# Pooled attention and a tanh-shrink MLP on one core: where the loads are queued, and who turns batch 1's keys and queries

## The chip, the core and the metric

The kernel runs on one core of one Trainium2 chip. A core has four compute engines, TensorE (matrix products, PE in the profile), VectorE (DVE), ScalarE (ACT) and GpSimd (POOL), and SyncE (SP), which here only issues DMAs. Each engine works through its own list of instructions in order and waits on semaphores for the others. SP, ACT and POOL can each issue DMAs; all of them are moved by the same 16 DMA engines. Data are worked on in SBUF (128 partitions), matrix products land in PSUM, which has 8 banks of 128 x 512 float32.

The metric is the time on the device in microseconds (us) of one execution. Before the change the median of three runs is 329.83 us (329.11 to 329.89).

## The reference

There are 8 batches, 8 heads, 576 positions and a head dimension of 64. Keys and values are averaged over groups of 8 positions, so there are 72 of them per head. The result of the attention, as 4608 rows of 512, goes through two weight matrices with `h - tanh(h)` between them.

```python
k_p = k.reshape(B, H, Sp, pool, D).mean(axis=3)
v_p = v.reshape(B, H, Sp, pool, D).mean(axis=3)
scores = scale * np.matmul(q, k_p.transpose(0, 1, 3, 2))
scores = scores - np.max(scores, axis=-1, keepdims=True)
attn = np.exp(scores)
attn = attn / (np.sum(attn, axis=-1, keepdims=True) + 1e-09)
attn_out = np.matmul(attn, v_p)
x = attn_out.transpose(0, 2, 1, 3).reshape(B * S, H * D)
h = x @ w_in            # 512 -> 2048
g = h - np.tanh(h)
out = g @ w_out         # 2048 -> 512
```

## The kernel before

**Tiling.** Of the 576 positions of a batch, 512 make four blocks of 128 queries (`s_block`, `av_block`), and the last 64 make a "tail"; the tails of two batches share one block of 128 (`s_tail`, `av_tail`). The MLP runs over nine groups of 512 rows: groups 0 to 7 are the blocks of batches 0 to 7, group 8 is the four blocks of tails. In each group the first product (`h_mms`, line 344, in group 0 `h_mm_pair`, line 363) makes 16 tiles h of 128 x 512; ScalarE takes tanh of each (line 355 or 375), VectorE subtracts (line 356 or 376) and writes gT. The second product (`o_mms`, line 384) makes four row blocks, each of 16 matmuls, in 16 units of four matmuls; a finished block is copied out of PSUM (`o_store`, line 403) and stored by SP.

**Attention of the next batch inside a group.** While group g is multiplied, the attention of batch g+1 is woven in by hand: the list `plan` says after which h tile (numbers below zero, -16 to -1) or o unit (0 to 15) each step stands. "s" is the scores of a block (`s_mms`, line 235, then the maximum and the subtraction on VectorE, lines 249 and 252); "e" is the exponential on ScalarE (line 260) and the turn of E into ET by a DMA on SP's queue (`e_turn_dma`, line 273); "a" is attention times values (`av_mms`, line 299), the division on VectorE (lines 317 and 318), and the turn of the block into xT by a DMA on SP's queue (line 327). Group 0 has its own weave, the loop `for u in range(16)`, with the scores of batch 1 behind units 3, 5 and 7 and the attention from unit 10 on.

**What a batch needs beforehand.** Its k, q and v are loaded as float32 (`load_list`). GpSimd adds the eight positions of a group of keys together (`pool_k`, lines 157, 160, 163, into kd), SP's queue turns kd into kT by DMA (line 200), GpSimd places kT into KB (`k_place_kT`, line 194); ScalarE casts q to bfloat16 (`q_cast`, line 208), and SP's queue turns it into qT by DMA (line 214). GpSimd pools v (`pool_v`, lines 172 to 184, into VB). The tail queries are loaded as float32 (`load_tail`, line 129), cast by GpSimd (line 571, for the first pair line 596) and turned by DMA (lines 590 and 598). From group 1 on, these loads stand on SP's queue, one behind each h tile (the list `todo`); those of k and q of batch 2 are on GpSimd's queue (lines 603 to 605), v and the tail of batch 2 on SP's (line 654).

**The start.** Batch 0's k comes in three pieces on SP's queue (rows 0 to 2, the last 64 rows, rows 2 to 4, in units of 128) and q in two halves on ACT's queue. `k_turn_pe`, `q_turn_pe`, `e_turn_pe` and `x_turn_pe` turn batch 0's tiles by TensorE, with a product by a unit matrix into PSUM and a copy out (lines 220, 485, 282, 336). `fill` (line 419) multiplies zeros, to no effect on the result. GpSimd casts the second half of q of batch 0. GpSimd's queue then carries the loads that cast to bfloat16 on the way: v of batch 0 (held until the 64-row piece of k has landed), the first weights w1 in four pieces (the first held until rows 2 to 4 of k have landed), the second weights w2 in four, and between them v of batch 1. SP's queue loads k, q and the tail of batch 1, held until the second piece of w1 has landed (line 470).

```python
after(load_rows(k_rows, k_raw[1], 1), w1_dmas[1])
load_q(1, q_raw[1])
load_tail(0)
```

**Order.** The order of each engine's instructions, and of each queue's DMAs, is the order in which the program writes them. An engine that waits holds up everything behind it.

Of the kernel before, what the change touches and what calls it, by code (L numbers as in the profile page):

```python
# [27 lines left out]
NT = 5  # L28
# [7 lines left out]
def kernel(  # L36
# [50 lines left out]
    tl_raw = [const.tile([128, H, D], FP32, name=f"tl_raw{i}") for i in range(2)]  # L87
# [39 lines left out]
    def load_tail(i, eng=None):  # L127
        for s in range(2):
            (eng or nc.sync).dma_start(
                out=tl_raw[i % 2][64 * s : 64 * s + 64, :, :],  # L130
                in_=q[2 * i + s, :, QA:S, :].rearrange("h p d -> p h d"),
            )

# [19 lines left out]
    def pool_k(b, eng, t0=0, t1=NT):  # L153
        r = k_raw[b % 2].rearrange("p t (j d) -> p t j d", d=D)[:, t0:t1, :, :]
        kd = kds[b % 2][:, t0:t1, :, :]
        n = t1 - t0
        eng.tensor_tensor(  # L157
            out=r[:, :, 0:4, :], in0=r[:, :, 0:4, :], in1=r[:, :, 4:8, :], op=ALU.add
        )
        eng.tensor_tensor(  # L160
            out=r[:, :, 0:2, :], in0=r[:, :, 0:2, :], in1=r[:, :, 2:4, :], op=ALU.add
        )
        eng.tensor_tensor(
            out=kd,
            in0=r[:, :, 0:1, :].to_broadcast([128, n, 2, D]),
            in1=r[:, :, 1:2, :].to_broadcast([128, n, 2, D]),
            op=ALU.add,
        )
# [258 lines left out]
    load_rows(k_rows, k_raw[0], 0, 0, 2)  # L427
# [42 lines left out]
    after(load_rows(k_rows, k_raw[1], 1), w1_dmas[1])  # L470
    load_q(1, q_raw[1])
    load_tail(0)


# [4 lines left out]
    def q_turn_pe(b, j, bank, eng):  # L479
        for m in range(NHP):  # L480
            turn(
                PS[:, bank, m * 128 : (m + 1) * 128],
                q_bf[b % 2][:, j, 2 * m : 2 * m + 2, :].rearrange("p h d -> p (h d)"),
            )
        eng(out=qTs[b % 2][:, j, :, :].rearrange("p m c -> p (m c)"), in_=PS[:, bank, :])
# [82 lines left out]
    def prepare(b):  # L568
        pool_k(b, nc.gpsimd)
        if b % 2:  # L570
            ge(out=tl_bf[(b // 2) % 2][:, :, :], in_=tl_raw[(b // 2) % 2][:, :, :])

    def load_list(b, eng):
        i = b % 2
        r = [
            lambda: load_rows(k_rows, k_raw[i], b, 0, 4, eng),
            lambda: load_rows(k_rows, k_raw[i], b, 4, NT, eng),
            lambda: load_q(b, q_raw[i], eng=eng),
            lambda: load_rows(v_rows, v_raw[i], b, 0, 4, eng),
            lambda: load_rows(v_rows, v_raw[i], b, 4, NT, eng),  # L580
        ]
        if b % 2 == 0:
            r.append(lambda: load_tail(b // 2, eng))
        return r

    def turns(b):
        k_turn_dma(b)
        q_turn_dma(b)
        if b % 2:
            nc.sync.dma_start_transpose(  # L590
                out=tl_T[(b // 2) % 2][:, :, :],
                in_=tl_bf[(b // 2) % 2].rearrange("p h d -> p (h d)"),
            )

    k_place_kT(1, ge)
    ge(out=tl_bf[0][:, :, :], in_=tl_raw[0][:, :, :])
    nc.gpsimd.memset(v_raw[0][64:128, 4, :], 0.0)
    nc.sync.dma_start_transpose(
        out=tl_T[0][:, :, :], in_=tl_bf[0].rearrange("p h d -> p (h d)")
    )  # L600


    for ld in load_list(2, nc.gpsimd)[:3]:
        ld()
# [20 lines left out]
    for u in range(16):  # L625
# [14 lines left out]
        if 10 <= u <= 12:  # L640
            a_unit(u - 10, av_block(1), (PB, PA, PB)[u - 10], (1, u - 10))
        if u == 12:
            k_turn_dma(2)
        if u == 13:
            av_mms(ets[3], av_block(1), PA)
            x3 = normalise(PA)
            s_unit(4, s_tail(0), PB)
        if u == 14:
            x_turn_pe(x3, 1, 3, 0, se)
            e_unit(4)  # L650
            tail0 = ets[4]
        if u >= 12:
            o_store(0, u % 4, OB[u % 4], (se, ve)[u % 2])
    for ld in load_list(2, nc.sync)[3:]:
        ld()
    nc.gpsimd.memset(v_raw[1][64:128, 4, :], 0.0)
    k_place_kT(2, ge)
# [6 lines left out]
    for g in range(1, NG):  # L664
# [4 lines left out]
        if nb is not None:  # L669
# [36 lines left out]
            if g > 1:  # L706
                pool_v(nb, nc.gpsimd)
# [15 lines left out]
        todo = load_list(nb + 1, nc.sync) if more else []  # L723
        for i in range(NHID):
            h_mms(g, i, i % 6)
            h_act(i, i % 6)
            if todo and (g > 1 or i > 4):
                todo.pop(0)()
            if g == 1 and i == 5:
# [3 lines left out]
            if g == 1 and i < 4:  # L733
                q_cast(2, se, i, i + 1)
            if g == 1 and i == 3:
# [48 lines left out]
```

## Time and profile before

| what | us |
|---|---|
| median of three runs | 329.83 |
| the profiled execution | 331.36 |
| its span, first to last instruction | 329.6 |
| TensorE busy | 298.8 (91% of the span) |
| VectorE busy | 191.6 (58%) |
| ScalarE busy | 149.8 (45%) |
| GpSimd busy | 108.2 (33%) |
| mean granted TensorE clock | 0.984 |

The profile is of one execution. In its chain of work that ended last, 55% of the span is TensorE and 36% is DMA, of which 12% is ET, 8% the loads of q, 6% qT and 4% xT. In the answers quoted below, a group or a row of the timeline has its start, its length, the engine, the line, and the tiles written and read (written<-read); "idle before" names what ended the wait. A row of the stages has the window, then the busy time of PE, PEld (weight loads of TensorE), DVE, ACT and POOL with the number of instructions, then the granted clock of TensorE (1.00 is full), the busy share of the DMA engines, and GB/s.

### The profile page before, as it was taken

To read this page: it belongs to the slowest core of one execution; us is meant where nothing else is said; L and a number is where in the kernel's file an instruction comes from. 1 tells how busy PE (TensorE), PEld (TensorE's weight loads), DVE (VectorE), ACT (ScalarE), POOL (GpSimd) and SP (SyncE) were. 2 spreads that over 40 slices of the span, in tenths; PEclk is the share of its full clock that TensorE was granted. 3 is DMA by queue.
4 is the path that set the end of the run, shared out by engine and by line. 5 is a ranking of instruction groups with operands and counts; after the bars stand their busy time and mean duration, and the time that the engine had idled before them with its cause. 6 is when DMAs were issued, how large, how long until landed. Compare 5 with 4: busy or idle time off the path is not lost.

```text
span 329.6 us, 4754 instructions
## 1 busy us (share of the span) xinstructions
PE 298.8 (91%) x1737; PEld 149.9 (45%) x1737; DVE 191.6 (58%) x315; ACT 149.8 (45%) x249; POOL 108.2 (33%) x94
## 2 busy tenths in 40 slices
PE   5879959899949799899999999999899989999995
PEld 1347824444415345444454444445444534444443
DVE  5576456578813398349735973696189627505700
ACT  3157452176331474447436733674265316425611
POOL 2831613711770565036707720574090000000000
PEclk9999997999978999999999999999999999999999
DMA  8999997889994899789968995998642360021023
GB/s 232 184 218 270 230 182 225 159 197 238 261 297 97 162 284 212 130 171 266 247 150 209 331 162 139 166 328 184 152 111 38 93 173 7 0 77 52 0 47 81
DMA packets 91735, 55.72 MB, mean 169 GB/s; under 512 B 65504, under 2 KB 79200, under 8 KB 91712
## 3 DMA queue, kind: packets, MB, share of 16 engines
q1 hardware_dynamic: 83440, 46.64, 59.8%
q0 software_dynamic: 6032, 7.60, 12.1%
q10 hardware_dynamic: 2240, 1.18, 1.4%
q8 instruction: 13, 0.21, 0.3%
q14 instruction: 10, 0.08, 0.1%
HBM read 36.70 MB, written 9.44 MB: 140 GB/s over the span
## 4 chain that ended last, share of the span: by engine, by line
PE 55%; DMA 36%; ACT 2%; SPq 2%; issue 1%; DVE 1%; POOL 0%; ACTq 0%
PE PS L344 26%; PE PS L384 24%; DMA ET<-E 12%; DMA q_raw<-in_q_dram 8%; DMA qT<-q_bf 6%; DMA xT<-x_sb 4%; PE PS L299 3%; DMA w1b<-in_moe_w_in_dram 3%; DMA k_raw<-in_k_dram 3%; PE PS L235 2%; ACT q_bf L208 1%; DMA out_dram<-o_sb 1%; SPq L118 1%; DVE mx L249 0%; SPq L405 0%
## 5 line engine op out<-in xcount | busy, mean ns | idle before, releaser
L384 PE MATMUL PS<-w2b,gT 128*128 128x512 bf16 (+2 forms) x592 | 138.1, 381 | 0.0
L356 DVE TENSOR_TENSOR gT<-PS,t_sb 128x512 bf16<-128x512 f32 x128 | 85.7, 689 | 53.0 <-ACT t_sb L355 52.3
L344 PE MATMUL PS<-xT,w1b 128*128 128x512 bf16 x448 | 99.8, 380 | 4.7 <-DMA xT<-x_sb 4.7
L355 ACT ACTIVATE t_sb<-PS 128x512 f32<-128x512 f32 x128 | 76.3, 597 | 39.7 <-PE PS L344 37.2
L384 PEld LDWEIGHTS <-gT 128*128 128x128 bf16 x592 | 55.1, 99 | 58.1 <-issue 3.8
L344 PEld LDWEIGHTS <-w1b 128*128 128x128 bf16 x512 | 49.3, 98 | 63.6 <-issue 6.7
L403 ACT COPY o_sb<-PS 128x512 f32<-128x512 f32 x33 | 19.3, 585 | 84.0 <-PE PS L384 84.0
L260 ACT ACTIVATE E<-sh 128x576 bf16<-128x576 f32 x36 | 24.2, 681 | 27.2 <-DVE sh L252 27.2
L194 POOL COPY KB<-kT 64x288 bf16<-64x288 bf16 x14 | 5.9, 422 | 90.4 <-DMA kT<-kd 73.1
L249 DVE TENSOR_REDUCE mx<-PS 128x8 f32<-128x576 f32 x36 | 27.1, 752 | 10.6 <-PE PS L235 10.5
L317 DVE RECIPROCAL rden<-PS 128x8 f32<-128x8 f32 x36 | 7.4, 206 | 41.4 <-PE PS L299 41.2
L157 POOL TENSOR_TENSOR k_raw<-k_raw 128x1280 f32<-128x1280 f32 x7 | 20.3, 2898 | 27.2 <-DMA k_raw<-in_k_dram 27.2
L299 PE MATMUL PS<-VB,ET 128*128 128x130 bf16 (+4 forms) x240 | 20.3, 227 | 9.5 <-DMA ET<-E 9.5
L252 DVE TENSOR_TENSOR sh<-PS,mx 128x576 f32<-128x576 f32 x36 | 27.3, 758 | 1.3
L318 DVE TENSOR_TENSOR x_sb<-PS,rden 128x512 bf16<-128x512 f32 x36 | 24.9, 692 | 1.4 <-DVE rden L317 0.2
L299 PEld LDWEIGHTS <-ET 128*128 128x128 bf16 (+1 forms) x240 | 15.7, 103 | 20.3 <-DMA ET<-E 14.4
L172 POOL TENSOR_TENSOR v_raw<-v_raw 128x1280 f32<-128x1280 f32 x6 | 17.4, 2902 | 9.9 <-DMA v_raw<-in_v_dram 9.5
L208 ACT CAST q_bf<-q_raw 128x1024 bf16<-128x1024 f32 (+1 forms) x19 | 16.5, 866 | 6.9 <-DMA q_raw<-in_q_dram 6.9
L235 PE MATMUL PS<-KB,qT 128*128 128x144 bf16 x128 | 13.3, 227 | 5.3 <-DMA qT<-q_bf 4.0
L363 PE MATMUL PS<-xT,w1b 128*128 128x256 bf16 x128 | 14.9, 273 | 1.5 <-DVE gT L376 0.8
L235 PEld LDWEIGHTS <-qT 128*128 128x128 bf16 x128 | 9.7, 98 | 13.6 <-DMA qT<-q_bf 5.5
L376 DVE TENSOR_TENSOR gT<-PS,t_sb 128x512 bf16<-128x512 f32 x16 | 10.6, 688 | 7.9 <-ACT t_sb L375 6.3
(66 smaller groups left out, 154.5 us busy)
## 6 DMA issues: line engine op xcount, KB each, us to landing
out_dram<-o_sb SPq DMA_DIRECT2D x32, 256.0 KB, 2.6
k_raw<-in_k_dram SPq DMA_DIRECT2D x6, 1024.0 KB, 6.9
q_raw<-in_q_dram SPq DMA_DIRECT2D x6, 1024.0 KB, 9.3
v_raw<-in_v_dram SPq DMA_DIRECT2D x6, 1024.0 KB, 11.6
w1b<-in_moe_w_in_dram POOLq DMA_DIRECT2D x4, 512.0 KB, 8.9
w2b<-in_moe_w_out_dram POOLq DMA_DIRECT2D x4, 512.0 KB, 23.1
k_raw<-in_k_dram SPq DMA_DIRECT2D x2, 512.0 KB, 6.2
q_raw<-in_q_dram ACTq DMA_DIRECT2D x2, 512.0 KB, 7.4
```

The source lines that it names most:

```text
L157: eng.tensor_tensor(out=r[:, :, 0:4, :], in0=r[:, :, 0:4, :], in1=r[:, :, 4:8, :], op=ALU.add)
L208: eng(out=q_bf[b % 2][:, j0:j1, :, :].rearrange("p j h d -> p h j d"), in_=q_raw[b % 2][:, :, j0:j1, :],)
L235: nc.tensor.matmul(PS[ps, banks[m // 2], KP * (m % 2) : KP * (m % 2) + KP], lhsT=qT[:, m, :], rhs=KB[kb][:, m, :], start=True, stop=True,)
L249: nc.vector.reduce_max(out=mx.rearrange("p k h o -> p k (h o)"), in_=sc, axis=AX.X)
L252: nc.vector.tensor_tensor(out=sh[:, :, :, :], in0=sc, in1=mx.to_broadcast([128, 2, 4, G]), op=ALU.subtract)
L260: nc.scalar.activation(out=E.rearrange("p t c -> p (t c)")[:, 0:NK], in_=sh.rearrange("p k h c -> p (k h c)"), func=ACT.Exp, scale=SCALE,)
L299: nc.tensor.matmul(PS[ps, banks[half], D1 * h : D1 * (h + s1 - s0)], lhsT=ET[:, t, c0 : c0 + (ps.stop - ps.start)], rhs=VB[kb][:, t, s0:s1 ...
L318: nc.vector.tensor_tensor(out=x_sb[:, :, :, :], in0=ps[:, :, :, 0:D], in1=rden.to_broadcast([128, 2, 4, D]), op=ALU.mult,)
L344: nc.tensor.matmul(PS[:, bank, c0:c1], lhsT=w1b[:, fb, i * 128 : (i + 1) * 128], rhs=xT_of(g)[:, fb, c0:c1], start=(fb == 0), stop=(fb == ...
L355: nc.scalar.activation(out=t_sb[:, :], in_=PS[:, bank, :], func=ACT.Tanh)
L356: nc.vector.tensor_sub(out=gT[:, i, :], in0=PS[:, bank, :], in1=t_sb[:, :])
L384: nc.tensor.matmul(PS[:, bank, 0 : c1 - c0], lhsT=gT[:, i, tb * 128 : (tb + 1) * 128], rhs=w2b[:, i, c0:c1], start=(i == 0), stop=(i == NH ...
```

## The change

1. *Start.* Batch 0's k rows 2 to 4 go second on SP's queue, the 64-row piece moves to ACT's queue behind the first half of q, and the second half of q moves from ACT's to SP's queue. v of batch 0 is held until rows 0 to 2 of k have landed, the first piece of w1 is held by nothing, the other three until VectorE has pooled batch 0's keys. ScalarE instead of GpSimd casts the second half of q, ahead of the key placement. The ten fill matmuls ahead of the last key turns become three.
2. *Batch 1.* Its k and q are loaded on GpSimd's queue, behind w1 and ahead of w2; v of batch 1, the last two pieces of w2 and the first tail follow behind the pooling of its keys. In group 0's first product ScalarE casts q behind pairs 6 to 9 (it was 4 to 7), TensorE turns q behind pairs 8 to 11 and k behind the last, ScalarE copies the turned q out, and VectorE and ScalarE place k. The DMAs that turned k and q of batch 1 and GpSimd's placement go.
3. *Tails.* `load_tail` casts on the way, on GpSimd's queue, straight into tl_bf; tl_raw and GpSimd's casts go.
4. *Group 0 and 1.* Block 2 of batch 1 is turned into xT by TensorE and ScalarE instead of by DMA. The tail scores move from unit 13 of group 0 to tile 2 of group 1, their exponential to tile 4, their attention from tile 5 to tile 10; the placement of batch 2's keys follows the tail scores; the casts of batch 2's q move from tiles 0 to 3 to tiles 4 to 7, and their turn from tile 3 to 7.
5. *Later batches.* All loads of a batch are issued on GpSimd's queue: those of batch 2 ahead of the pooling of its keys in group 0, those of batch 3 behind the pooling of v of batch 2, and from group 2 on ahead of the pooling of v at the start of the group.

```diff
-    k0 = load_rows(k_rows, k_raw[0], 0, 4, NT)
+    k0 = load_rows(k_rows, k_raw[0], 0, 0, 2)
+    k0 += load_rows(k_rows, k_raw[0], 0, 4, NT, nc.scalar)
     k0 += load_rows(k_rows, k_raw[0], 0, 2, 4)
-    load_q(0, q_raw[0], 2, 4, nc.scalar)
+    load_q(0, q_raw[0], 2, 4)
...
     after(load_rows(v_rows, v_bf[0], 0, eng=nc.gpsimd), k0[0])
     w1_dmas = [load_w1(0)]
-    after(w1_dmas, k0[1])
-    w1_dmas.append(load_w1(1))
-    q_cast(0, ge, 2, 4)
-    for c in range(2, 4):
-        w1_dmas.append(load_w1(c))
-    load_w2(0)
-    load_w2(1)
-    load_rows(v_rows, v_bf[1], 1, eng=nc.gpsimd)
-    load_w2(2)
-    load_w2(3)
-    after(load_rows(k_rows, k_raw[1], 1), w1_dmas[1])
-    load_q(1, q_raw[1])
-    load_tail(0)
...
-    pool_k(0, nc.vector, 2, 4)
+    pooled = pool_k(0, nc.vector, 2, 4)
+    for c in range(1, 4):
+        w1_dmas.append(load_w1(c))
+        if c == 1:
+            after(w1_dmas[1:], pooled)
+    load_rows(k_rows, k_raw[1], 1, eng=nc.gpsimd)
+    load_q(1, q_raw[1], eng=nc.gpsimd)
+    load_w2(0)
+    load_w2(1)
     q_cast(0, se, 0, 2)
+    q_cast(0, se, 2, 4)
...
-    fill(10, 7)
+    fill(3, 7)
...
     pool_k(1, nc.gpsimd)
-    k_turn_dma(1)
+    load_rows(v_rows, v_bf[1], 1, eng=nc.gpsimd)
+    load_w2(2)
+    load_w2(3)
+    load_tail(0)
...
-        if 4 <= m < 8:
-            q_cast(1, se, m - 4, m - 3)
-        if m == 7:
-            q_turn_dma(1)
+        if 6 <= m < 10:
+            q_cast(1, se, m - 6, m - 5)
+        if 8 <= m:
+            q_turn_pe(1, m - 8, m % 2, se)
+    kps = flat(0, NT * 128)
+    k_turn_pe(1, 0, NT, kps)
+    k_place(1, kps[:, 0:NK], (ve, se))
...
-    for ld in load_list(2, nc.gpsimd)[:3]:
+    for ld in load_list(2, nc.gpsimd):
         ld()
...
+        if u == 11:
+            turn_tail(0)
         if u == 12:
+            av_mms(ets[2], av_block(1), PB)
+            x2 = normalise(PB)
             k_turn_dma(2)
         if u == 13:
             av_mms(ets[3], av_block(1), PA)
             x3 = normalise(PA)
-            s_unit(4, s_tail(0), PB)
+            x_turn_pe(x2, 1, 2, 2, se)
...
             if g > 1:
+                if more:
+                    for ld in load_list(nb + 1, nc.gpsimd):
+                        ld()
                 pool_v(nb, nc.gpsimd)
...
-        todo = load_list(nb + 1, nc.sync) if more else []
-            if todo and (g > 1 or i > 4):
-                todo.pop(0)()
-            if g == 1 and i == 5:
+            if g == 1 and i == 2:
+                s_mms(s_tail(0), PAIRS[0])
+                tail0 = s_shift(PAIRS[0])
+                k_place_kT(2, ge)
+            if g == 1 and i == 4:
+                tail0 = e_turn_dma(s_exp(tail0))
+            if g == 1 and i == 10:
                 av_mms(tail0, av_tail, PAIRS[0])
                 x_turn_dma(normalise(PAIRS[0]), B, 0)
                 pool_v(nb, nc.gpsimd)
-            if g == 1 and i < 4:
-                q_cast(2, se, i, i + 1)
-            if g == 1 and i == 3:
+                for ld in load_list(nb + 1, nc.gpsimd):
+                    ld()
+            if g == 1 and 4 <= i < 8:
+                q_cast(2, se, i - 4, i - 3)
+            if g == 1 and i == 7:
                 q_turn_dma(2)
```

More of the change, by code (lines that the diff above doesn't have):

```diff
@@ L86 @@
     VB = [const.tile([128, NT, 3, D1], BF16, name=f"VB{i}") for i in range(2)]
-    tl_raw = [const.tile([128, H, D], FP32, name=f"tl_raw{i}") for i in range(2)]
     tl_bf = [const.tile([128, H, D], BF16, name=f"tl_bf{i}") for i in range(2)]
@@ L125, in load_q, with load_tail, turn_tail @@
         )
-    def load_tail(i, eng=None):
+    def load_tail(i):
         for s in range(2):
-            (eng or nc.sync).dma_start(
-                out=tl_raw[i % 2][64 * s : 64 * s + 64, :, :],
+            nc.gpsimd.dma_start(
+                out=tl_bf[i % 2][64 * s : 64 * s + 64, :, :],
                 in_=q[2 * i + s, :, QA:S, :].rearrange("h p d -> p h d"),
             )
+    def turn_tail(i):
+        nc.sync.dma_start_transpose(
+            out=tl_T[i % 2][:, :, :], in_=tl_bf[i % 2].rearrange("p h d -> p (h d)")
+        )
     def load_w1(c):
@@ L162, in pool_k @@
         )
-        eng.tensor_tensor(
+        return eng.tensor_tensor(
             out=kd,
@@ L484, in q_turn_pe @@
             )
-        eng(out=qTs[b % 2][:, j, :, :].rearrange("p m c -> p (m c)"), in_=PS[:, bank, :])
+        eng(out=qTs[b][:, j, :, :].rearrange("p m c -> p (m c)"), in_=PS[:, bank, :])
     def v_pool_pe(b, bank):
@@ L582, in load_list @@
         if b % 2 == 0:
-            r.append(lambda: load_tail(b // 2, eng))
+            r.append(lambda: load_tail(b // 2))
         return r
@@ L589, in turns @@
         if b % 2:
[L590 to L596, printed above, removed]
+            turn_tail(b // 2)
     nc.gpsimd.memset(v_raw[0][64:128, 4, :], 0.0)
-    nc.sync.dma_start_transpose(
-        out=tl_T[0][:, :, :], in_=tl_bf[0].rearrange("p h d -> p (h d)")
-    )
-    for ld in load_list(2, nc.gpsimd)[:3]:
+    for ld in load_list(2, nc.gpsimd):
         ld()
@@ L639 @@
             v_place(1, v_pool_pe(1, 0), nc.vector)
-        if 10 <= u <= 12:
-            a_unit(u - 10, av_block(1), (PB, PA, PB)[u - 10], (1, u - 10))
+        if 10 <= u <= 11:
+            a_unit(u - 10, av_block(1), (PB, PA)[u - 10], (1, u - 10))
+        if u == 11:
+            turn_tail(0)
         if u == 12:
+            av_mms(ets[2], av_block(1), PB)
+            x2 = normalise(PB)
             k_turn_dma(2)
```

8 lines of the change are left out of this document (removed).

## The prediction

> **What bounds the kernel now.** I read the page first: TensorE is busy 91% of a 329.6 us span, the DMA row stands at 8 and 9 up to slice 26. So TensorE is the bound on average, and what a change can win is TensorE's idle time and its time at half clock. The waits of TensorE between 40 and 110 us say where that is (total, times, longest):
>
> ```profile
> PE PS L299 <- DMA ET<-E: 6.4, 2, 4.8
> PE PS L235 <- DMA qT<-q_bf: 3.8, 2, 3.5
> PE PS L344 <- DMA xT<-x_sb: 2.8, 2, 2.1
> PE PS L363 <- DVE gT L376: 0.8, 1, 0.8
> ```
>
> The first matters most: attention of the next batch waits for its turned exponentials (ET), and before that its scores wait for the turned queries (qT). The chain in order of time shows what makes them late in group 0:
>
> ```profile
> 20.96 18.88 DMA q_raw<-in_q_dram
> ...
> 43.52 6.56 DMA qT<-q_bf
> 50.08 0.05 issue
> 50.13 0.44 PE PS L235 x4
> ...
> 52.88 8.77 DMA ET<-E
> ```
>
> Batch 1's queries take 18.9 us to land, since SP's queue shares the DMA engines with the weights; ScalarE's cast of them holds up the tanh behind it (3.5 us in its waits), and the turn by DMA takes 6.6. The stages show the second price, the granted clock (column PEclk) after a long wait:
>
> ```profile
> 50.10:54.30 4.20, 4.17 (x20) 1.98 (x21) 2.94 (x4) 1.35 (x2) 2.17 (x3) 0.59 0.62 206
> 54.30:58.50 4.20, 4.20 (x29) 2.36 (x27) 3.10 (x5) 1.13 (x3) 0.66 (x1) 1.00 1.06 298
> 96.90:101.30 4.40, 4.32 (x17) 2.09 (x18) 0.90 (x2) 0.00 (x0) 0.15 (x1) 0.50 0.66 181
> ```
>
> After the waits of 3.5 and 4.8 us the clock is at half; after one of 1.6 us (at 61.7) it is not. The timeline gives the durations that the sum uses:
>
> ```profile
> 8.78 4.45 PE L419 MATMUL PS<-zeros 128*128 128x512 bf16 x10
> 11.57 1.95 DVE L163 TENSOR_TENSOR kd<-k_raw 128x256 bf16<-128x256 f32 x1
> 12.15 1.07 POOL L208 CAST q_bf<-q_raw 128x1024 bf16<-128x1024 f32 x1
> 14.79 1.07 ACT L485 CAST qT<-PS 128x512 bf16<-128x512 f32 x2
> 43.38 2.08 ACT L375 ACTIVATE t_sb<-PS 128x512 f32<-128x512 f32 x4
> 50.64 3.57 PE L384 MATMUL PS<-w2b,gT 128*128 128x512 bf16 x8
> 54.30 1.89 PE L384 MATMUL PS<-w2b,gT 128*128 128x512 bf16 x8
> ```
>
> **The change, part by part.** Marks of the run before: scores of batch 0 at 15.4, first o product 42.8, scores of batch 1 at 50.1, their attention 61.7, group 1 at 69.0, group 2 at 109.9.
>
> *Ramp.* The last k rows move up to second on SP's queue, and the 1.95 us pooling step that ran beside GpSimd's cast (0.42 us for the same shape at 6.08) loses its neighbour: pooled keys are ready near 10 instead of 13.5. But ScalarE now casts the second half of batch 0's queries (1.04) ahead of the key placement (0.39) and the first eviction (0.55), and that half is third on SP's queue while v and the first weights, no longer held back until 7.8 and 10.6, already flow. Its landing is not in the trace. The third load on SP's queue landed at 10.4; batch 1's queries, twice as big and shared with GpSimd's loads, took 18.9, so half of that from 6.5, when v's bytes can first flow, is 16. I take 12.5, nearer the first, as most bytes ahead are the same; scores then start at 14.5, one us early. Seven fills fewer leave TensorE colder there: ten took 4.45 (0.43 each cold, about 0.2 warm), so the eight v-pooling matmuls (1.25) and three fills (0.8) may cost double, some 1.5 to 2 us, partly under VectorE's softmax. Net 0, from 2 lost to 1.5 won.
>
> *Batch 1 turned by TensorE.* q of batch 1 now stands behind w1 and ahead of w2 in one queue; by bytes (v, w1, k and q are about 7.5 MB read, at the 350 to 400 GB/s of busy stretches) it lands near 30, before its first cast at 36.5 (pairs of the second half are 0.89 apart from 31.2). So the 3.5 us wait of ScalarE and the 0.8 of TensorE go. New on ScalarE from then: 6 tanh, 4 casts and 4 evictions, at 0.52 each (four took 2.08) 7.3 us from 37.4 to 44.7; the last key turn waits for the last eviction, since both use banks 0 and 1. TensorE's 16 query and 5 key turns (0.4 us for four or five in the timeline, about 1.9 in all) lie within that. First o product 45.0, so 2.2 later than before; but scores follow after four o units (0.865 each) at 48.4 instead of 50.1: 1.7 won. The wait of 3.5 is gone and with it the half clock: 3.57 minus 1.89, 1.7 won. The key placement (DVE and ScalarE, 0.45) hides under those units.
>
> *First ET.* Issued 2.75 after the scores as before (50.13 to 52.88), at 51.2. TensorE's order reaches attention 8.3 us after the scores (61.7 less 1.6 wait, less 50.1, less 1.7 cold): 56.7. ET takes 2.4 alone, 8.8 before, with k and q of batch 2 in flight: landing 53.6 to 60.0. The loads of batch 2 are now issued behind the pooling of k and the last weights, at some 37 to 45 on GpSimd's queue, and should be in at 55 to 57; I take 57.7. Attention 4.0 early, so 0.6 of it from here.
>
> *Rest of group 0.* The third block's turn by TensorE and ScalarE removes the wait of 0.65 for its DMA at the group's end, costs 0.25 on TensorE; the tail scores (0.45) move into group 1. Group 1 starts 4.85 early.
>
> *Group 1.* The qT wait (0.4) goes: no load flows while it turns, and six h tiles (5.2 us) cover its 4.4. Tail scores cost 0.45 here; their softmax on VectorE and ScalarE and the later casts are absorbed by six banks of slack. Loads of batch 3 come after pooled v, which waits for the tail attention at tile 10; 3.4 MB at 360 GB/s are 9.5 us, from about 15 after the group's start to 24.5. ET is issued at about 17.5, attention is reached at 23. Before, ET was queued behind those loads on SP (9.2 us, wait 4.8). Now, beside them on another queue, bounds 2.4 and 9.2; I take 8, as the nearest row is the 8.8 beside loads of GpSimd's queue. Wait 2.6, too short for half clock: 2.2 of wait won, and 1.7 (8 matmuls, 3.6 to 1.9) plus 0.5 (two attention blocks at half clock) won. Net 4.3. The wait for xT at its end stays: three o units behind a turn of 3.3.
>
> *Groups 2 to 6.* Loads leave SP's queue and are issued by GpSimd ahead of pooled v: 4 to 5 us of issue time there (0.79, 0.56, 0.95 per load in the rows of batch 2). GpSimd idles 12 to 18 us per group before the key placement, and VB is ready 14 us into the group, needed at 20: no cost. The first ET is no longer behind loads; waits for ET after 110 are 3.1 in four, of which the two behind loads (0.7 and 0.6) go. 1.0 won, from 2 lost to 3 won. Casting the tail by the load removes four GpSimd casts (0.6 each), all in idle time: 0.
>
> Sum: 0 + 4.85 + 4.3 + 1.0 = 10.2. The profiled execution took 331.36 (span 329.6 and 1.8 around it), which gives 321.2; it lies 1.5 above the median 329.83 of the runs shown, so I forecast **319.6** for the median.
>
> **Rivals.**
>
> *Loads hold the turns up wherever they are queued.* For it: 8.77 us for an ET on SP's queue while the loads were on GpSimd's. Then the first attention comes at 60.0 and group 1 keeps its 4.8 and its cold stretch: only 1.7 and 0.85 and little else remain, 327.3. Against it: before, those loads were issued only 2 us ahead of ET; now they are nearly done in group 0. The Trainium skill, DMA: Bandwidth & Descriptors, section "Issuing engines are not separate DMA queues", speaks for this rival: transfers of all issuing engines interleave on the same 16 DMA engines, and spreading them saves issue time alone. Chance 0.15.
>
> *Turns share at once.* If ET beside loads takes about twice its 2.4, near 5, it lands before attention is reached in both groups: 1.0 and 2.6 more, 316; with a good ramp 314.5. Against it stands the 8.77. The same page, section "Queues, rings and completion order", would have it so: each DMA engine goes round the queues that have work, packet by packet. Chance 0.2.
>
> *Slower: the loads catch qT in every group.* GpSimd issues them right after the key placement, at 111.7 in group 2, and qT landed at 113.75. In batch 2's loads bytes flowed 2.1 us after the issue, so the first at 113.8: a hair behind. If loads were earlier than the end of qT, by the hold seen for ET the scores (due 6.2 us into the group) would wait until the loads are in, at 13.5, with a cold stretch of 1.7: 9 us in each of groups 2 to 5, 36, less the 10: 355; half as often, 337. It decides at about 1 us. For it: nothing else keeps loads off. Against it: qT is issued 1.3 after kT in every group, and the placement waits for kT. Chance 0.08.
>
> **How the numbers follow.** Likeliest case 0.53 (317 to 323); turns held 0.15; sharing at once 0.2; slower by caught qT 0.08; the rest, 0.04, is held turns with a ramp lost by 3 us or more, half of it level and half slower. A measurement tells 0.3%, 1 us, from no change. The first three are faster, 0.88; same 0.02, slower 0.10. Range 314.5 to 327.5: from sharing at once with a good ramp to held turns, which leaves out about 0.17.
>
> **What would show it.** Right: no wait of ScalarE for q_raw after 30, scores of batch 1 near 48, no half-clock stretch at 50 or 97, first o product some 2 us later than before, ET's landings in groups 2 to 6 under 8. Wrong: an L235 wait on qT in the later groups, ET beside loads still at 9 with half clock near 92, or ScalarE's second cast in the ramp starting after 15.

## The result and the profile after

The changed kernel takes 333.5 us (median; 330.09 to 337.95), and the kernel before, run beside it, 330.56 (328.27 to 332.1): a ratio of 1.0061, interval 1.0035 to 1.0086. It is slower by about 2 us where 10 us of gain were forecast, and lies above the range. The profiled execution of the changed kernel took 335.73 (span 333.9); it, the second profiled one below (337.6) and that of the kernel with batch 2's q, v and tail behind the pooling (337.2) are slow executions of their kernels, which the ratios leave out, so their profiles can hold waits that the median does not.

The marks of the two profiles, in us, beside what the prediction's steps make of them:

| mark | before | predicted | after |
|---|---|---|---|
| scores of batch 0 | 15.4 | 14.5 | 13.1 |
| first o product | 42.8 | 45.0 | 42.35 |
| scores of batch 1 | 50.1 | 48.4 | 45.8 |
| attention of batch 1 | 61.7 | 57.7 | 59.0 |
| group 1 starts | 69.0 | 64.2 | 67.7 |
| group 2 starts | 109.9 | 100.8 | 108.8 |
| group 3 starts | 143.0 | - | 146.9 |
| end of the span | 329.6 | 319.4 | 333.9 |

Up to the scores of batch 1 the change wins more than forecast, 4.3 instead of 1.7. Then it gives back 1.6 before their attention, 1.4 more by group 1, and group 2 takes 38.2 instead of 33.1. From group 3 on the two are within 0.4 us of each other (187.0 against 186.6). The start, from the timeline of the changed kernel (columns as before): the second half of q is cast at 10.18, the last keys are pooled at 10.66, and the scores start at 13.11.

```profile
10.18 1.05 ACT L212 CAST q_bf<-q_raw 128x1024 bf16<-128x1024 f32 x1 [1.83 <-DMA q_raw<-in_q_dram]
10.66 0.42 DVE L167 TENSOR_TENSOR kd<-k_raw 128x256 bf16<-128x256 f32 x1
...
13.11 0.91 PE L239 MATMUL PS<-KB,qT 128*128 128x144 bf16 x8
...
42.35 3.61 PE L388 MATMUL PS<-w2b,gT 128*128 128x512 bf16 x15
...
59.02 0.84 PE L303 MATMUL PS<-VB,ET 128*128 128x130 bf16 x6 [4.63 <-DMA ET<-E]
```

The waits of TensorE between 40 and 125 us after (total, times, longest) answer the four lines shown of before, which are the same for that window. The wait on DVE's gT (L363 before) is gone and the one for xT has shrunk from 2.8 to 1.0; but the one for ET has grown from 6.4 with 4.8 the longest, and the one of 3.5 for qT has merely moved from batch 1's scores to group 2:

```profile
PE PS L303 <- DMA ET<-E: 10.6, 2, 6.0
PE PS L239 <- DMA qT<-q_bf: 3.5, 2, 3.3
PE PS L348 <- DMA xT<-x_sb: 1.0, 1, 1.0
```

The chain in order of time (start, length, what) shows the three places. An ET takes 2.4 alone, a qT 4.3; here they take 10.0, 11.6 and 9.4:

```profile
45.96 0.52 PE PS L239 x8
...
49.02 9.96 DMA ET<-E
58.97 0.05 issue
...
85.61 11.56 DMA ET<-E
97.17 0.05 issue
...
108.84 9.40 DMA qT<-q_bf
118.24 0.05 issue
118.29 0.43 PE PS L239 x4
```

The stages (columns as before) show that the half clock behind batch 1's scores is gone, and that each of the three waits is now followed by one:

```profile
45.80:49.60 3.80, 3.66 (x26) 2.02 (x25) 2.81 (x4) 0.68 (x1) 1.41 (x2) 1.00 1.37 338
...
59.00:63.20 4.20, 4.18 (x19) 2.29 (x20) 1.80 (x4) 0.00 (x0) 0.00 (x0) 0.50 0.88 139
...
97.20:101.40 4.20, 3.96 (x15) 1.96 (x17) 0.90 (x2) 0.00 (x0) 0.00 (x0) 0.50 0.65 180
...
118.30:122.50 4.20, 4.20 (x15) 1.75 (x16) 2.21 (x3) 0.94 (x2) 3.96 (x4) 0.59 0.90 179
```

How a turn becomes so long can be seen in group 2. qT is issued at 108.84 on SP's queue (q1 below) and the load of batch 4's keys 2.24 later on GpSimd's (q0). The DMA view of a window gives packets, MB and the time the packets took as a share of the 16 engines. In the changed kernel, from 112.5 to 113.5, only the turn moves, in packets under 512 bytes:

```profile
DMA packets 1131, 0.29 MB, mean 290 GB/s; under 512 B 1131, under 2 KB 1131, under 8 KB 1131
...
q1 hardware_dynamic: 1131, 0.29, 127.3%
```

From 114 to 116, with the load's packets there, the same view of the same kernel reads:

```profile
DMA packets 154, 0.61 MB, mean 305 GB/s; under 512 B 5, under 2 KB 5, under 8 KB 154
...
q0 software_dynamic: 149, 0.61, 99.1%
q1 hardware_dynamic: 5, 0.00, 0.1%
```

The five packets of the turn's queue carry 0.00 MB: the turn has no data left to move. From 109.7 to 113.9 the view reads

```profile
q1 hardware_dynamic: 2048, 0.52, 109.4%
```

and 0.52 MB is the whole qT (128 x 2048 values of two bytes). Its data had gone by 113.9, yet it counts as landed only at 118.24, just before the first load (118.58). A qT without loads near it lands 0.5 to 0.7 behind its last packet of data, this one 4.4. So this turn was caught in its last half us, not in its middle.

A turn that is issued when loads already flow is late in another way. In the packets of the trace, the first ET of group 0, issued at 49.02, begins to move at 53.75, 4.7 behind its issue, where a turn alone begins 1.2 behind it. Then it gets about one packet for each of the loads'; but its packets hold 256 bytes and most of the loads' 4096. From 54 to 57:

```profile
q0 software_dynamic: 266, 0.93, 92.1%
q1 hardware_dynamic: 270, 0.07, 12.9%
```

The Trainium skill, DMA: Bandwidth & Descriptors, section "Queues, rings and completion order", has each DMA engine go round the queues that have work, packet by packet, and has the signal that ends a transfer land only behind all earlier writes of its DMA engine, those of other queues too. The first fits the 266 and 270, the second the late landing of qT; that they are the cause is not shown, and the 4.7 us before ET's first packet stay open.

### The profile page after: what moved, and what is told of

Same layout as the page of the kernel before. It is cut to its first block, busy times and chain, and to the rows that moved or that the text cites. A ratio compares the mean times of both kernels' runs of the same rounds, so it can differ in the third digit from the quotient of the medians.

```text
span 333.9 us, 4749 instructions
## 1 busy us (share of the span) xinstructions
PE 297.9 (89%) x1725; PEld 151.6 (45%) x1755; DVE 190.3 (57%) x316; ACT 153.9 (46%) x256; POOL 130.5 (39%) x125
## 3 DMA queue, kind: packets, MB, share of 16 engines
q0 software_dynamic: 15728, 28.58, 35.6%
## 4 chain that ended last, share of the span: by engine, by line
PE 67%; DMA 19%; DVE 5%; ACT 4%; issue 2%; SPq 0%; ACTq 0%; DVEq 0%
PE PS L348 29%; PE PS L388 28%; DMA ET<-E 12%; PE PS L303 4%; DMA qT<-q_bf 3%; DMA xT<-x_sb 2%; DMA k_raw<-in_k_dram 2%; PE PS L239 2%; PE PS L367 2%; PE PS L224 1%; ACT E L264 1%; DVE sh L256 1%; DVE mx L253 1%; DVE x_sb L322 1%; ACT t_sb L379 1%
## 5 line engine op out<-in xcount | busy, mean ns | idle before, releaser
L388 PE MATMUL PS<-w2b,gT 128*128 128x512 bf16 (+2 forms) x576 | 135.8, 380 | 1.4 <-issue 0.7
L359 ACT ACTIVATE t_sb<-PS 128x512 f32<-128x512 f32 x128 | 76.2, 597 | 44.3 <-PE PS L348 41.3
L198 POOL COPY KB<-kT 64x288 bf16<-64x288 bf16 x12 | 5.0, 421 | 85.7 <-DMA kT<-kd 39.5
L303 PE MATMUL PS<-VB,ET 128*128 128x130 bf16 (+4 forms) x240 | 20.8, 230 | 13.1 <-DMA ET<-E 13.0
L212 ACT CAST q_bf<-q_raw 128x1024 bf16<-128x1024 f32 (+1 forms) x20 | 17.5, 876 | 6.4 <-DMA q_raw<-in_q_dram 6.4
## 6 DMA issues: line engine op xcount, KB each, us to landing
v_raw<-in_v_dram POOLq DMA_DIRECT2D x6, 1024.0 KB, 14.5
```

The source lines that it names most:

```text
L303: nc.tensor.matmul(PS[ps, banks[half], D1 * h : D1 * (h + s1 - s0)], lhsT=ET[:, t, c0 : c0 + (ps.stop - ps.start)], rhs=VB[kb][:, t, s0:s1 ...
L359: nc.scalar.activation(out=t_sb[:, :], in_=PS[:, bank, :], func=ACT.Tanh)
L388: nc.tensor.matmul(PS[:, bank, 0 : c1 - c0], lhsT=gT[:, i, tb * 128 : (tb + 1) * 128], rhs=w2b[:, i, c0:c1], start=(i == 0), stop=(i == NH ...
```

## The experiments

The theory to test, Q in the later expectations: a turn that is in flight when loads of another queue begin to flow, or is issued behind them, lands about when those loads do; what counts is which turn that is and how soon TensorE needs it. Rivals: GpSimd's queue itself is the trouble; the losses are those of groups 0 and 1 alone; another part of the change costs the time. Each ratio is to the kernel before, run beside it.

**Loads of later batches back on SP's queue.** From the changed kernel, batch 2's loads staying on GpSimd's:

```diff
-                if more:
-                    for ld in load_list(nb + 1, nc.gpsimd):
-                        ld()
...
+        todo = load_list(nb + 1, nc.sync) if more else []
...
+            if todo and (g > 1 or i > 7):
+                todo.pop(0)()
```

> The changed kernel, with k, q and v of batches 3 to 7 loaded on SP's queue again, one behind each h tile (the tail stays on GpSimd's queue). Theory H, that loads on GpSimd's queue hold the turns on SP's queue up: the turn of q in group 2 lands after 4.3 us again instead of 9.4, so its wait of 3.5 and the half clock behind it go, about 5 us; the later groups as in the kernel before; group 0 keeps its late ET. 326 to 328, ratio 0.985 to 0.995. Theory R, that any load in flight holds turns up alike, whatever queue it is on, and the loss in group 2 comes from loads issued 2 to 3 us earlier than before: the same gain here, since these loads are late again. Theory S, that the loss lies in what moved in groups 0 and 1: still at 331 to 333.

Measured: 326.68 us, 0.9873 [0.9834, 0.9913]. Group 2 takes 32.7 instead of 38.2, group 1 38.5 instead of 41.1. The first ET of group 0 still takes 9.79 and costs 4.5, since batch 2's loads stayed. So the move of the later loads to another queue (part 5) turns a gain of 1.3% into a loss. It moves them in time as well: group 2's first load is issued 5.3 behind qT here and 2.2 in the changed kernel, so this run alone does not tell the queue from the time. On the tile qT between 100 and 240 us, this kernel's answer (landing after issue, least, median, most) has none caught:

```profile
DMA to landing us min/median/max: 4.3/4.4/5.4
```

**Only k of batch 2 ahead of the first ET.** From the kernel of the run before:

```diff
-    for ld in load_list(2, nc.gpsimd):
+    for ld in load_list(2, nc.gpsimd)[:2]:
         ld()
...
+    for ld in load_list(2, nc.sync)[2:]:
+        ld()
```

> As the last, and of batch 2 only k is loaded ahead of the first ET (on GpSimd's queue); q and v follow on SP's queue behind group 0. H and R alike: the first ET lands in about 3 us instead of 10, the attention of batch 1 comes when TensorE reaches it (near 54 instead of 59) and without half clock behind it, another 5 to 7 us: 320 to 322, ratio 0.965 to 0.978. S: no more than 1 us.

Measured: 324.03, 0.9797 [0.9762, 0.9831]. The first ET lands 2.48 after its issue, without a wait or half clock, and group 1 starts at 62.0 instead of 67.7: what batch 1's scores had won now reaches group 1. But the time is 2 us above the 320 to 322 expected: q and v of batch 2, now behind group 0 on SP's queue, hold the tail's ET for 6.93 (wait 3.2), and group 1's first ET takes 7.92 (wait 3.3). The chain of this kernel:

```profile
68.39 6.93 DMA ET<-E
...
85.62 7.92 DMA ET<-E
```

**The kernel before, with its later loads on GpSimd's queue.** One part of the change alone:

```diff
+                if more:
+                    for ld in load_list(nb + 1, nc.gpsimd):
+                        ld()
                 pool_v(nb, nc.gpsimd)
...
-        todo = load_list(nb + 1, nc.sync) if more else []
```

> The kernel before with one part of the change alone: loads of batches 3 to 7 on GpSimd's queue, ahead of the pooling of v. H and R: turns of q or the first ET are caught in groups 1 to 5, 3 to 8 us slower than before, ratio 1.01 to 1.025. S: within 1 us of before.

Measured: 334.58, 1.0114 [1.0082, 1.0146]: this part alone makes the old kernel slower too. Its price is in ETs: the chain has one of 11.55 in group 1 (91.74 to 103.29), and group 2 takes 35.6 instead of 33.1 with a first ET of 12.54. From group 2 on no qT is caught (the longest takes 4.5), so a caught qT isn't needed for a loss.

**The same loads on ScalarE's queue.** From the first of these kernels:

```diff
-        todo = load_list(nb + 1, nc.sync) if more else []
+        todo = load_list(nb + 1, nc.scalar) if more else []
```

> As the first, but the loads of batches 3 to 7 stand on ScalarE's queue, which is not SP's and not GpSimd's, one behind each tanh from the group's start. H, that it is GpSimd's queue: the turns beside these loads land sooner than beside GpSimd's, ET in 4 to 6 us where it was 9 to 11; ratio within 0.5% of the first. R, any queue: ET beside the loads takes 9 to 11 again and the turn of q in group 2 is caught if loads flow before its end, ratio 1.0 or above.

Measured: 354.42, 1.0721 [1.0671, 1.077]. It isn't GpSimd's queue: ScalarE's is worse, because the loads then start at the first tiles of the group, beside qT. The waits and the tile qT of this kernel between 100 and 240 us:

```profile
PE PS L239 <- DMA qT<-q_bf: 24.7, 5, 10.5
```

```profile
DMA to landing us min/median/max: 8.0/9.2/10.6
```

In group 1 its qT, issued at 77.79, took 14.96. Two pairs say it without a model: with a load 1.4 us behind it on the same queue (the run with k alone ahead, 75.15 and 76.56) a qT takes 4.31; with a load 1.3 us behind it on ScalarE's queue (114.53 and 115.86) it takes 7.96, of which up to 1.2 is peculiar to group 2 (see the end), and with one 0.8 behind it in group 3 (150.12 and 150.89) 9.42.

**Loads between the turns.** From the kernel with only k ahead:

```diff
-    for ld in load_list(2, nc.sync)[2:]:
-        ld()
+    load_list(2, nc.sync)[2]()
...
                 tail0 = e_turn_dma(s_exp(tail0))
+                for ld in load_list(2, nc.sync)[3:]:
+                    ld()
...
-            if todo and (g > 1 or i > 7):
+            if todo and i < (3, 11)[g == 1] and (g > 1 or i > 7):
                 todo.pop(0)()
...
+            if u == (0, 3)[g == 1]:
+                for ld in todo:
+                    ld()
```

> Starts from the kernel with batch 2's q and v behind group 0 on SP's queue (324.03 us) and moves three pieces on that queue: v of batch 2 behind the tail's ET in group 1; of the later batches k and q stay ahead of the first ET, v goes behind the second one (unit 0, in group 1 unit 3). Theory Q (a turn that shares its flight with loads comes in with them, on any queue; what counts is how many bytes are in flight when it is issued): the tail's ET in group 1 lands in about 2.5 us instead of 6.9 and its wait of 3.57 goes, the first ET of group 1 lands in 3 to 4 instead of 7.9 and its wait of 3.68 goes, and with them the half clock behind each, 1.7 and 1.4; group 2 starts near 95 instead of 104.7; the first ETs of groups 2 to 5 land in 6 to 8 instead of 10.4. The execution takes 311 to 315. Theory R (an ET of the attention is slow because the queues carry about as many bytes at any time, and order on the queue changes nothing): ETs stay at 7 to 10, 320 to 325.

Measured: 327.42, 0.9915 [0.9887, 0.9944]: worse than the kernel it started from, so my expectation fell. Group 2's first ET is shorter (7.45 instead of 10.47), but it had slack; v behind the second ET then holds the third and fourth and the xT, which have none (TensorE's longest waits before an attention: 3.0 in group 1, then 1.5, 0.7, 1.2 and 1.9). From group 1 on, the chain of this kernel has later ETs, such as

```profile
89.78 6.48 DMA ET<-E
...
127.22 4.00 DMA ET<-E
```

Mere thinning of loads ahead of one turn isn't the aim; the bytes have to pass somewhere, and the turn that they pass in front of must have slack.

**The start alone.** The kernel before with part 1 of the change:

```diff
-    k0 = load_rows(k_rows, k_raw[0], 0, 4, NT)
+    k0 += load_rows(k_rows, k_raw[0], 0, 4, NT, nc.scalar)
...
-    load_q(0, q_raw[0], 2, 4, nc.scalar)
+    load_q(0, q_raw[0], 2, 4)
...
+    pooled = pool_k(0, nc.vector, 2, 4)
...
+    q_cast(0, se, 2, 4)
...
-    fill(10, 7)
+    fill(3, 7)
```

> The kernel before with part 1 of the change alone (the start), and batch 1's k, q and tail still on SP's queue behind the second piece of w1. The scores of batch 0 come at 13.1 instead of 15.4 in any case. Theory A (what comes after hangs on TensorE's order): all later marks move 2 earlier, 328.5. Theory B (the arrival of batch 1's queries on SP's queue, at 39.8 before, sets the scores of batch 1, and their load still waits for the second piece of w1): the scores of batch 1 stay within 1 us of 50.1, and the time is 330 to 331.

Measured: 329.37, 0.9974 [0.9939, 1.001]; span 327.6 against 329.6. The scores of batch 0 come 2.1 earlier, the first o product 1.7, the scores of batch 1 1.6, group 1 1.7. It is between the two theories and nearer to A: q of batch 1 is still held by the second piece of w1, but that piece comes earlier too. The chain of this kernel:

```profile
11.58 6.65 DMA w1b<-in_moe_w_in_dram
...
19.27 18.85 DMA q_raw<-in_q_dram
...
41.80 6.68 DMA qT<-q_bf
```

So the start is worth 1.6 to 2 us in the profile and about 1 us in the ratio, which cannot be told from no change; it is no part of the loss.

**Without the loads of batches 4 to 7.** From the changed kernel:

```diff
             if g > 1:
-                if more:
-                    for ld in load_list(nb + 1, nc.gpsimd):
-                        ld()
                 pool_v(nb, nc.gpsimd)
```

> The changed kernel without the loads of batches 4 to 7: their attention works on what already lies in the tiles. Theory Q (the loads of GpSimd's queue hold up the turns of groups 2 to 5): group 2 takes 33 us instead of 38.2, no wait for qT there, first ETs of groups 2 to 5 land in 2.4 to 4 instead of 9 to 10, and the waits of about 1 us in each of those groups go: 324 to 326, groups 0 and 1 as they were. Rival (groups 2 to 5 are slowed by something else that came with the change, GpSimd's or ScalarE's work): 330 or more.

Measured: 328.97, 0.9961 [0.9923, 0.9998]. Group 2 takes 33.2 instead of 38.2, groups 3 to 5 take 30.2, 32.9 and 30.1 instead of 31.0, 33.1 and 30.7. That is Q's account, 6.6 us in these four groups, of which 5.0 are group 2's. The total fell by 4.3 only, to 3 us above the expected 326: 2.1 of that stands in groups 6 and 7, which have no loads in either kernel and took 33.6 and 29.3 instead of 33.2 and 27.6. TensorE stands for 2.1 before group 7, after which the granted clock is 0.57 for 4 us; in the changed kernel it stands for 1.7 and the clock stays full. What makes that wait longer is open. On the tile ET between 100 and 240 us this kernel reads

```profile
DMA to landing us min/median/max: 2.4/2.4/4.3
```

where the changed kernel has 2.4/2.9/10.4.

**The changed kernel again.** No edit; for a second profile.

> The changed kernel itself, for a second profile. If the load of batch 4 catches qT of group 2 by the order in which the kernel writes them, the wait of about 3.5 us for qT in group 2 stands again, and none for qT in groups 3 to 5; if it was chance, it is gone or comes in another group. The waits of 4.6 and 6 for the first ETs of groups 0 and 1 stand in any case. 332 to 334.

Measured: 333.31, 1.008 [1.0045, 1.0116]. The first ETs take 11.17 and 11.53, and qT of group 2 is caught once more, 9.30, with the load issued 2.25 behind it; in groups 3 to 5 the gap is 2.1 to 2.2 and no qT is caught, as in the first profile. So it is no accident of one execution, though two traces do not show that every execution has it.

**Later loads 2.9 us later on GpSimd's queue.** From the changed kernel:

```diff
+        for ld in lds:
+            ld()
         eng.tensor_tensor(
             out=r[:, :, 0:2, :], in0=r[:, :, 0:2, :], in1=r[:, :, 2:4, :], op=ALU.add
         )
...
-                if more:
-                    for ld in load_list(nb + 1, nc.gpsimd):
-                        ld()
-                pool_v(nb, nc.gpsimd)
+                pool_v(nb, nc.gpsimd, load_list(nb + 1, nc.gpsimd) if more else [])
```

> The changed kernel, with one thing moved: from group 2 on GpSimd issues the loads of the next batch behind the first addition of the pooling of v instead of ahead of it, 2.9 us later. Theory Q: the loads of group 2 then come some 1 us behind the landing of its qT (4.4 after its issue) instead of 2.2 after its issue, so that its wait of 3.5 and the half clock behind it go; the ETs of these groups stay at 9 to 12: 333.3 less 5.1, 328.2, group 2 in 33 to 34. Rival (qT of group 2 is late for another reason, such as the stores and turns ahead of it on SP's queue): group 2 stays at 38, 333.

Measured: 331.54, 1.0017 [0.9982, 1.0051]. In the profile group 2 takes 33.1 instead of 38.2, as Q said; its qT takes 5.5 and isn't waited for:

```profile
DMA to landing us min/median/max: 4.3/4.3/5.5
```

Part of it comes back in group 3 (32.1 instead of 31.0, an ET 11.6 after its issue). The ratio fell by 0.4 to 0.6%, 1.5 to 2 us, less than half of the 5.1, and the intervals overlap; the time is 3 us above Q's 328.2. Unprofiled executions leave no trace, so whether qT is caught in every one of them stays open.

**And batch 2's q, v and tail behind the pooling of its k, all still on GpSimd's queue.** From the kernel of the run before:

```diff
-    for ld in load_list(2, nc.gpsimd):
+    for ld in load_list(2, nc.gpsimd)[:2]:
         ld()
     prepare(2)
+    for ld in load_list(2, nc.gpsimd)[2:]:
+        ld()
```

> The run before with one more move: q, v and the tail of batch 2 stand on GpSimd's queue behind the pooling of its k instead of ahead of it; every load stays on GpSimd's queue. Theory Q (place, not queue): the first ET of group 0 lands in 2.5 to 3 instead of 9.6, no wait and no half clock there, group 1 starts near 62 instead of 67.7; the loads of batch 3 are still in flight with the first ET of group 1, whose wait of 4 to 6 stays: 328.2 less 5.7, 322.5. Rival (GpSimd's queue itself slows the turns, so that only a move to SP's queue mends it): 327 or more.

Measured: 332.55 as the median of four executions, 325.72, 327.89, 337.2 and 337.4; the ratio, 0.9888 [0.9824, 0.9951], is that of the two short ones, some 326.7, and the profile that of the 337.2. The time is thus near the rival's 327 and does not decide between the two. The first ET lands in 2.59 and isn't waited for, as Q said, on the queue that the rival blamed. But in the profile the loads, issued at 56.67, met the next turns: the xT issued at 55.67 took 2.40, the one issued at 56.95 took 10.52, and group 1 waits 7 us for it and starts at 67.6 after all. The chain of this kernel:

```profile
56.95 10.52 DMA xT<-x_sb
...
86.93 13.54 DMA ET<-E
```

My 322.5 had left out that there is always a next turn; this one is issued 0.3 us on the wrong side of the loads' issue. Whether the two short executions escape it is not traced.

**v a group later.** From the kernel with only k of batch 2 ahead (324.03):

```diff
-    for ld in load_list(2, nc.gpsimd)[:2]:
+    for ld in load_list(2, nc.gpsimd)[:3]:
...
+                if nb > 2:
+                    load_rows(v_rows, v_raw[nb % 2], nb)
                 pool_v(nb, nc.gpsimd)
...
+        todo[3:5] = []
...
-            if todo and (g > 1 or i > 7):
+            if todo and (g > 1 or i > 4):
...
                 tail0 = e_turn_dma(s_exp(tail0))
+                for ld in load_list(2, nc.sync)[3:]:
+                    ld()
...
-            if g == 1 and 4 <= i < 8:
-                q_cast(2, se, i - 4, i - 3)
-            if g == 1 and i == 7:
+            if g == 1 and i < 4:
+                q_cast(2, se, i, i + 1)
+            if g == 1 and i == 3:
```

> Starts from the kernel with only k of batch 2 ahead of the first ET (324.03 us, loads of later batches on SP's queue). q of batch 2 is back ahead of the first ET, behind k on GpSimd's queue, so that its casts and its turn stand at tiles 0 to 3 of group 1 again; v of batch 2 goes behind the tail's ET; of batch 3 on, k and q are issued a group ahead as before and v at the start of the group that pools it. Theory Q (a turn comes in with the bytes in flight when it is issued; what counts is that no turn that TensorE soon needs is issued behind them): q adds 1 MB, 3 us, so the first ET of group 0 lands near 55 and costs a wait of about 1; the tail's ET takes 2.5 and the first ET of group 1 lands before its attention or up to 1 after it; group 1 takes 35 to 37 instead of 42.7, and the execution 317 to 320. Rival, after the miss of the run with loads between the turns (the 10 us that a batch's loads take on the queue come out of TensorE's time in group 1 wherever they stand): group 1 stays at 40 to 43, 323 to 327.

Measured: 318.72, 0.9628 [0.9576, 0.9679], the best of all and within Q's 317 to 320. Group 1 takes 34.6 instead of 42.7. The first ET of group 0 lands at 55.19, behind q, for a wait of 0.8; group 1's lands 5.50 after its issue, and TensorE does not wait for it. The chain of this kernel, then its waits:

```profile
49.11 6.08 DMA ET<-E
...
70.07 2.57 DMA ET<-E
...
80.53 5.50 DMA ET<-E
```

```profile
PE PS L303 <- DMA ET<-E: 5.4, 6, 1.9
```

and the granted clock of its page stays at 9 from the third slice to the end:

```profile
PEclk9599999999999999999999999999999999999999
```

It keeps parts 1 to 4 of the change, but for the place of batch 2's casts and turn of q. It has each later batch's loads on SP's queue, behind the turns issued earlier, and loads v at the start of the group that pools it, where the ETs have slack. These moves were not tried one by one.

## Why the prediction was wrong, step by step

- *Ramp.* Its net of 0 was the wrong size: 2.3 won. The second half of q landed at 10.2 in place of 12.5, although v and the first weights were already under way, and the seven fills fewer cost nothing that the marks show.
- *Batch 1 turned by TensorE.* Right. Set against a ramp 2.3 earlier, the first o product is 1.9 later than before (2.2 predicted) and the scores of batch 1 are 2.0 earlier (1.7 predicted). The half clock there is gone. TensorE's two waits of 0.6 for ScalarE's copies (at 41.3 and 42.3) are the price, as said.
- *First ET.* This step failed. I wrote that the loads of batch 2 "should be in at 55 to 57" and gave ET 6.5 us; it took 9.96. The last of v landed at 58.2 and the tail at 60.7. GpSimd's own issue stood still twice until a piece of w2 was in, which put off the second piece of v and the tail; but the first piece of v was issued ahead of that, at 42.08, and was still 15.9 us under way. GpSimd's timeline:

```profile
42.08 0.77 POOL L111 DMA_DIRECT2D v_raw<-in_v_dram  x1
44.68 0.54 POOL L117 DMA_DIRECT2D v_raw<-in_v_dram  x1 [1.82 <-DMA w2b<-in_moe_w_out_dram]
47.18 1.41 POOL L128 DMA_DIRECT2D tl_bf<-in_q_dram  x2 [1.96 <-DMA w2b<-in_moe_w_out_dram]
```

  TensorE reached the attention at 54.4, so the wait was 4.6 and not 1, and brought a half clock that the step did without. The run with only k ahead shows both gone.
- *Rest of group 0.* The term for the missing xT wait can't be read by itself; group 1 started 1.3 early, not 4.85. Of the 3.55 missing, 1.3 is the attention at 59.0 in place of 57.7, and about 2.1 the half clock behind it (two o units of 1.90 where a warm one is 0.86); both belong to the step above.
- *Group 1.* Failed: net 4.3 won predicted, nothing measured (41.1 against 41.0). I took 8 for an ET beside loads, "as the nearest row is the 8.8"; it took 11.56, above both bounds, issued 5.1 us behind the first of batch 3's loads (80.53), and it landed 0.3 behind the last of them (96.84). Those loads were under way for 16.3 us, where I had 9.5. The wait was 6.0 and not 2.6, and the half clock at 97 came back; that 2.6 would be too short for one was read into the gap between rows of 1.6 and 3.5 (see the end).
- *Groups 2 to 6.* Failed: 1.0 won predicted, 5.4 lost. Some 5 of it is the caught qT of group 2, the mechanism of the rival that I gave 0.08, in one group of four; I priced it at 9 a group, it cost 3.3 of wait and 1.7 of half clock in this profile, while issuing the loads later won only 1.5 to 2 us in the ratio. The margin that I called a hair was the right place to look: the load is issued 2.1 to 2.25 behind qT in all four groups. In groups 3 to 5 its first packet comes 3.9 to 4.2 after qT's issue, and qT, landing at 4.3 to 4.4, has just passed; in group 2 it comes at 4.9, and there qT takes 5.5 even when the loads come 2.9 us later. That group 2 has this longer qT was not to be seen in the profile before.
- *The rivals.* "Loads hold the turns up wherever they are queued" (327.3) was near on the first attention, 59.0 against its 60.0, and on group 1's wait, 6.0 against 4.8. With one caught qT, 5.1, added after the result, it gives 332.4, 1 us below the 333.5. "Turns share at once" fell with the ETs of 9.96 and 11.56, where it had about 5: the turn does share, but packet for packet against larger ones, and only after standing for 4.7. The Trainium skill, DMA: Bandwidth & Descriptors, section "Issuing engines are not separate DMA queues", says that spreading transfers over engines saves issue time alone. It spoke rightly against the change, but the queue does matter here, for it sets what a load must stand behind: the same loads at the same places of the program give 0.9873 on SP's queue, where group 2's begin 5.3 us behind qT's issue, and 1.0721 on ScalarE's, where they begin 1.3 behind it.

The error behind all three failed steps is one: I priced a turn beside loads as a slower turn, and took the queue as a matter of issue time. In the kernel before, from group 2 on, the loads stood on the turns' own queue behind qT, which landed in 4.3 to 4.5. Two slips of reading and sum change nothing: the DMA row up to slice 26 also holds 4 to 7, and the sum gives 319.7, not 319.6.

## What to carry to other kernels

Price a DMA turn that meets loads of another queue near the landing of those loads, not at a multiple of its own time (here up to 13.5 us for an ET of 2.4, and 15.0 for a qT of 4.3), and look at which turn is in flight 2 to 5 us behind each load's issue. On the turns' own queue, loads issued 1.3 to 1.4 us behind a turn left it at its 2.4 to 2.6 (ET) or 4.3 (qT) in these profiles; moving loads to an idle queue gives that up. Where bytes must pass, put them in front of the turn with the most slack, and check the turn after it as well.

## What was not expected of the hardware

- A turn can have moved all its data and still not be landed: the caught qT counts as landed 4.4 us behind its last packet of data, and 4.3 in the second profile. A turn issued behind loads stands for 4.7 us before its first packet (4.8 for group 1's first ET) and then gets about one packet for each of theirs. Whether that hangs on the size of the loads' packets was not tried.
- In group 2 of the kernels made from the changed one, qT needs 4.9 to 5.5 us even with no load near it, for it pauses by itself. The DMA view of the changed kernel from 108.8 to 118.3, in 40 slices of 0.24 us, shows 1.4 us of pause from the tenth slice on, before the first load's packet at 113.75:

```profile
DMA  9991469990000009999998932999899899999916
```

  The kernel before has no such pause there (qT 4.28), and SP takes 3.4 us over this issue where it takes 1.3 to 2.0 elsewhere in the changed kernel. Without the pause qT would have passed. One packet of an instruction queue lies at 109.92, within this qT, and in the second profile at 113.26, within its qT again, while in the kernel before it lies at 115.36, behind qT. Over all profiles, from group 2 on, every qT with such a packet (16 KB, queue q8) in its first 2 us took at least 4.7: eleven of them, eight with no load near, 4.74 to 5.50. Without such a packet and without loads, qT took 4.28 to 4.46. In the kernel with the start alone the packet (206.18) falls into the qT of group 5, which takes 4.74, while that of group 2 takes 4.29. That it is the cause was not tried.
- A wait need not be 3.5 us long to bring a half clock. In the kernel with loads between the turns TensorE waited 2.1 for qT and the stage behind it reads 0.66:

```profile
79.40:82.40 3.00, 3.00 (x13) 1.30 (x14) 2.97 (x5) 1.00 (x3) 2.84 (x3) 0.66 1.02 360
```

  while 1.9 in the best kernel was followed by full clock. Over all profiles, from 30 us on, no wait of 1.4 to 1.92 was followed by a lowered clock within 4.5 us, and of those from 1.94 on all were but one (2.12, ahead of group 2 in the kernel before).
